# An order of instructions kept as a table in place of a scheduler with offsets

## Chip, core and metric

The kernel runs on one core of a Trainium2 chip. The metric is device time in microseconds (us) of one execution. The core's engines run their own instruction streams side by side: PE (TensorE, matmuls), DVE (VectorE), ACT (ScalarE), POOL (GpSimd) and SP (SyncE, which here issues most DMAs). They wait for one another through semaphores.

## The reference

The kernel computes one layer and its backward pass: the output and the gradients of all eight inputs, for x of 2 batches × 4000 tokens × 144 channels in bfloat16. The forward function:

```python
xa = _layernorm(x)
q, k, v = split(einsum('btd,de->bte', xa, w_qkv))
p = softmax(einsum('btd,bsd->bts', q, k) * D ** (-0.5))
glob = einsum('bts,bsd->btd', p, v) @ w_att_out
u, g = split(gelu(xa @ w_mlp_in))
gc = depthwise_conv5(_layernorm(g), dw_csgu)
loc = (u * gc) @ w_mlp_out
m = concatenate([glob, loc])
m = m + depthwise_conv5(m, dw_merge)
return x + m @ w_merge
```

The attention is full: 4000 × 4000 scores for each batch. `reference` calls `jax.vjp` of this function with `grad_out` and returns the output and all gradients.

## The kernel before

Tokens are handled in 32 blocks of 125 (PB = 125, NB = 32) for each batch. The kernel's stages in order of the span are:

- the head (class `Head`: weights are loaded, transposed and folded together; `pre_pieces`: layer norm of the tokens of batch 0 and transposes, L399 to L446), until about 57 us;
- the attention rows of batch 0 (`phase_att`), 57 to 585 us. For each of the 32 row blocks t it makes the scores S (L1664 with 128 partitions of contraction and L1670 with the remaining 16) in PSUM tiles `ps`, takes each row's minimum and copies the scores out (DVE, L1688 and L1690), takes the exponential (ACT, L1696), transposes it with DMA, and multiplies with V: Y (L1720, 32 matmuls into the PSUM tile `yz`). The DVE and ACT then read `yz`: `rl` (L1726), `dj` (L1729), `nd` (L1731), `yn` (L1733), `ty` (L1736). The gradient of the scores is made from a second product (L1706, or L1709 and L1711), stored transposed by DMA (L1891), and multiplied in Z (L1766, again into a tile `yz`) and X (L1811, accumulated by DVE in L1817). There is one buffer for `yz`. The projections of each row are made ahead of it (`pj`, L1623 to L1629), and their transposes come by DMA (L1646) into `qt`;
- between them, the local branch of the layer (`local_units`, L486 to L690, with matmuls L521 and L522 for the hidden units and L553 and L556 for their gradients), cut into small units;
- the merge of batch 0 (585 to 680 us; weight gradient `Hps` L2096, transposes L2017 and L2022 of reloaded rows `Yg` and `Yr`, outputs `po` L2193 and L2195 with the copies L2196 and the stores L2197), beside which the head pieces of batch 1 run (transposes L399 to L446 again);
- the attention rows of batch 1, until 1210 us, then its merge and the final weight gradients (`pg` L2401, DVE L2408 to L2416, transposes `fpt` L2418, stores L2265, L2414 and L2423).

The Python functions emit all operations in a source order. After that, `Planner.plan` takes the emitted instructions, joins PE instructions that write the same PSUM tile into groups (at most 16; the score matmuls in groups of up to 8), and fixes an order of the groups for each engine. It pins that order by a dependence between each instruction and the next one of its engine:

```python
for e in E:
    prev = None
    for g in order[e]:
        for i in groups[g]["ins"]:
            if prev is not None:
                self.tc.add_manual_dep(i, prev.name, ..., reason="planned order")
            prev = i
```

Before, `order` comes from a list scheduler in `plan`. It holds a duration for every kind of instruction (`cost`), works out which groups must follow which (`region`, `meet`, `under`), and goes through modelled time: whenever an engine is free, it takes among its ready groups the one with the smallest key. The key is the group's place in the source order plus an offset of its kind, `LEAD[tag.engine.tile]`, a list of several hundred numbers.

Matmuls on a zero tile, which nothing reads (`warm`, L153, in `Head.loads`; WARM = 190 of them), have the largest key and so fill moments in which the schedule has no other PE work. They stand from 3 to 57 us of the span.

## Time and profile before

| | before |
|---|---|
| median of 3 runs | 1300.91 us |
| lowest, highest | 1298.82, 1301.12 us |
| profiled execution | 1301.75 us |
| its span | 1299.9 us |
| mean granted TensorE clock | 0.993 |
| instructions in the span | 39018 |
| DMA | 186.53 MB, mean 143 GB/s |

The span is the time between the first and the last record of the profiled execution; its own time is 1.85 us longer. "Busy" is the time in which an engine works; PEld is PE's loading of weights, which overlaps its matmuls. A row of the waits view has the engine and line that waited, the one that released it, the us in total, the number of times and the longest. A row of the timeline has start, duration, engine, line, operation, tiles out and in, and in brackets the idle time before it with its releaser. In the table by stretch, each engine has its busy time and, in brackets, its instructions. The clock is the share of full TensorE speed that was granted.

### The profile page before, as it was taken

The numbers are of one execution on the slowest core, as the hardware profiler recorded it, in microseconds if no ns is written. First come the engines' busy times: TensorE is split into PE (matmuls) and PEld (weight loads), VectorE is DVE, ScalarE is ACT, GpSimd is POOL, SyncE is SP. The second block draws the span as 40 slices with busy tenths as digits, with TensorE's granted clock in tenths as the row PEclk, the third lists the DMA queues.
The fourth block names the chain that finished last, engine by engine and source line by source line (L and its number), as shares of the span: only waits on it lengthen the run. The fifth ranks groups of instructions, "written<-read, shape, count | busy, mean of one in ns | idle before, by whom it ended". The sixth has DMA issues, their size and how long they took to land. (4 is left out here: it accounts for less than half of the span.)

```text
span 1299.9 us, 39018 instructions
## 1 busy us (share of the span) xinstructions
PE 1261.1 (97%) x15888; PEld 1046.4 (80%) x15888; DVE 1051.9 (81%) x2825; ACT 755.4 (58%) x1232; POOL 488.0 (38%) x971
## 2 busy tenths in 40 slices
PE   8999999999999999999999999999999999999996
PEld 7777888778888878888877788888878788878995
DVE  7589888988898978779668988888889798887744
ACT  4766656665566665536645656666565665554471
POOL 8443333444344333313623333434334343222130
PEclk9999999999999999999998999999999999999998
DMA  4499898988989997984249898988898888888511
GB/s 123 79 160 160 157 153 152 146 155 154 154 149 149 157 154 138 171 204 113 74 96 168 150 161 145 155 154 154 143 164 137 159 146 153 157 147 178 162 56 54
DMA packets 630207, 186.53 MB, mean 143 GB/s; under 512 B 612336, under 2 KB 624971, under 8 KB 630021
## 3 DMA queue, kind: packets, MB, share of 16 engines
q1 hardware_dynamic: 629271, 183.57, 78.1%
q8 instruction: 124, 2.03, 0.6%
q14 instruction: 56, 0.46, 0.1%
q0 software_dynamic: 208, 0.25, 0.1%
q10 hardware_dynamic: 548, 0.21, 0.1%
HBM read 20.82 MB, written 14.22 MB: 27 GB/s over the span
## 5 line engine op out<-in xcount | busy, mean ns | idle before, releaser
L1688 DVE TENSOR_SCALAR_CACHE_REDUCE Pb<-ps 125x1000 bf16<-125x1000 f32 x256 | 306.6, 1198 | 82.9 <-PE ps L1670 79.2
L1696 ACT ACTIVATE Pb<-Pb,nm 125x1000 bf16<-125x1000 bf16 x256 | 277.8, 1127 | 104.8 <-DVE nm L1690 104.3
L1811 PE MATMUL X<-SX 125*125 125x144 bf16 x2048 | 294.3, 229 | 3.2 <-ACT l_fl L650 0.9
L1811 PE MATMUL X<-SX,Pb 125*125 125x144 bf16 x2048 | 289.0, 226 | 0.0
L1709 ACT CAST SX<-ps 125x1000 bf16<-125x1000 f32 x189 | 187.8, 994 | 170.8 <-PE ps L1670 168.9
L1811 PEld LDWEIGHTS <-SX 125*125 125x125 bf16 x2048 | 259.0, 137 | 26.9 <-issue 26.7
L1664 PE MATMUL ps<-xaT_m,qt 128*125 128x500 bf16 x1024 | 262.3, 376 | 4.5 <-DVE Pb L1688 2.2
L1811 PEld LDWEIGHTS <-Pb 125*125 125x125 bf16 x2048 | 260.1, 137 | 4.9 <-issue 4.6
L1817 DVE TENSOR_TENSOR acc<-X,acc 125x432 f32<-125x432 f32 x372 | 200.8, 550 | 23.9 <-PE X L1811 21.3
L1766 PE MATMUL yz<-xa_aug,SX 125*125 125x144 bf16 x2048 | 153.0, 230 | 5.9 <-ACT ty L1736 3.7
L1664 PEld LDWEIGHTS <-qt 128*125 128x125 bf16 x1024 | 122.4, 137 | 44.7 <-issue 5.5
L1766 PEld LDWEIGHTS <-SX 125*125 125x125 bf16 x2048 | 141.1, 139 | 13.2 <-issue 9.8
L1720 PE MATMUL yz<-xa_aug,SX 125*125 125x145 bf16 x2048 | 143.4, 228 | 0.9 <-DMA SX<-Pb 0.9
L1711 DVE TENSOR_TENSOR SX<-SX,Pb 125x1024 bf16<-125x1024 bf16 x189 | 132.0, 699 | 13.9 <-ACT SX L1709 9.8
L1720 PEld LDWEIGHTS <-SX 125*125 125x125 bf16 x2048 | 135.7, 137 | 3.6 <-issue 2.0
L1670 PEld LDWEIGHTS <-qt 16*125 16x125 bf16 x1024 | 36.6, 128 | 99.8 <-issue 99.8
L1670 PE MATMUL ps<-XR,qt 16*125 16x500 bf16 x1016 | 112.1, 421 | 0.0
L1706 DVE TENSOR_TENSOR SX<-ps,Pb 125x1000 bf16<-125x1000 f32 x67 | 80.1, 1196 | 11.6 <-ACT SX L1709 8.6
L651 POOL TENSOR_TENSOR A_dwc<-l_fl,A_dwc 128x512 f32<-128x512 f32 (+2 forms) x48 | 37.6, 784 | 97.6 <-ACT l_fl L650 97.5
L1744 POOL TENSOR_SCALAR SX<-qz,rl 125x144 bf16<-125x144 bf16 x62 | 24.3, 392 | 114.9 <-DVE rl L1726 113.4
L1639 POOL COPY qz<-qz 125x48 bf16<-125x48 bf16 x124 | 35.2, 310 | 71.9 <-ACT qz L1629 71.7
L633 POOL TENSOR_SCALAR l_w<-gd,nc,c 125x144 f32<-125x144 bf16 x64 | 29.4, 467 | 83.1 <-DVE c L631 83.0
(485 smaller groups left out, 2334.3 us busy)
## 6 DMA issues: line engine op xcount, KB each, us to landing
go_h<-in_grad_out_dram SPq DMA_DIRECT2D x4, 567.0 KB
Yg<-ug_d SPq DMA_DIRECT2D x4, 567.0 KB
Yn_d<-yn SPq DMA_DIRECT2D x64, 35.2 KB
Zn_d<-qz SPq DMA_DIRECT2D x64, 35.2 KB
ug_d<-ugr SPq DMA_DIRECT2D x32, 70.3 KB
SX<-in_x_dram SPq DMA_DIRECT2D x16, 140.6 KB
out_dram<-Pb SPq DMA_DIRECT2D x16, 140.6 KB
out_dram<-SX SPq DMA_DIRECT2D x16, 140.6 KB
```

Source lines behind the costliest of these rows:

```text
L651: nc.gpsimd.tensor_tensor(acc, fl[0:rows, 0:n], acc, op=ALU.add)
L1664: mm = nc.tensor.matmul(pp[r // 2][:, r % 2, 0:CH], QT[i][:, 3 * h, 0:PB], xaTm[:, c * CH:(c + 1) * CH], start=True, stop=False)
L1670: nc.tensor.matmul(pp[r // 2][:, r % 2, 0:CH], QT[i][rs, 1 + h, 0:PB], xr, start=False, stop=True)
L1688: nc.vector.tensor_scalar(pv(Pbuf, i % NPB, c2), src, -1.0, 3.0e38, op0=ALU.mult, op1=ALU.min, accum_out=NM[i][:, c2:c2 + 1])
L1696: nc.scalar.activation(v, v, ACT.Exp, bias=NM[i][:, 4:5], scale=-1.0)
L1706: nc.vector.tensor_tensor(pv(Sbuf, i % NDB, c2), src, pv(Pbuf, i % NPB, c2), op=ALU.mult)
L1709: nc.scalar.copy(pv(Sbuf, i % NDB, c2), src)
L1711: nc.vector.tensor_tensor(sc, sc, pchunk(i % NPB, c2), op=ALU.mult)
L1720: nc.tensor.matmul(Y, PT[0:PB, j, 0:PB], xaa[:, j, 0:D + 1], start=(j == 0), stop=(j == NB - 1))
L1766: nc.tensor.matmul(Z, ST[0:PB, j, 0:PB], xaa[:, j, 0:D], start=(j == 0), stop=(j == NB - 1))
L1811: nc.tensor.matmul(X[:, jj, :], l, r, start=(n_ == 0), stop=(n_ == len(ops) - 1))
L1817: nc.vector.tensor_tensor(av, X[:, 0:nj, :], av, op=ALU.add)
```

## The change

The scheduler goes: `cost`, `port`, `under`, `region`, `meet`, the table `LEAD` and the constants COLD and RING that it used. In its place stands `ORDER`, which has for each of the five engines the list of its groups in the order in which they are to run. The list is written as differences between the numbers of successive groups. The grouping and the pinning stay as they are. WARM becomes 111 in place of 190. No other operation is added, removed or changed, and the order was found by moving single operations.

```diff
-COLD = 8.5
-WARM = 190
-RING = 230
+WARM = 111
...
-LEAD = {}
+ORDER = {}
 for _s in """
-Fdwct A.Pb:9742 D.Pb:2821 D.jf:-16178 P:-219 S.out_5_dram:13749
-Fdwit A.Pb:2671 D.Pb:-1680 P:1687 S.out_4_dram:8143
...
+PE 10 1 1 1 1 1 1 1 1 1 1 1 1 1 1 1 1 1 1 1 1 1 172 3 -174 1 1 1 174 2 11 -186 ...
...
+    _e, *_v = _s.split()
+    ORDER[_e] = list(itertools.accumulate(int(_a) for _a in _v))
...
-    def plan(self, i0, i1, window=700):
-        import heapq
+    def plan(self, i0, i1):
...
-        key = [g["x"] + LEAD.get(g["cls"], 0.0) + (1e9 if (g["t"] or "")[:4] == "warm" else 0.0) for g in groups]
...
-                    free_t[e] = s + w + G["d"]
...
-        self.groups, self.order, self.times = groups, order, times
+        assert len(groups) == sum(len(v) for v in ORDER.values())
+        order = ORDER
+        for e in E:
+            assert sorted(order[e]) == [x for x, g in enumerate(groups) if g["e"] == e]
+        self.groups, self.order = groups, order
```

Where the two orders differ, set side by side: of the 79 warm matmuls that are gone, 27 stood ahead of the first layer norm transposes L441 (17.34 us in the profile before), 27 stood between 46.02 and 50.21 us, and 25 elsewhere in the head.

## The prediction, made before the changed kernel ran

> **What bounds the kernel now.** I read the busy shares first, then stretches of the span by stage, then the waits of PE (TensorE), and last the timeline at the places where those waits lie. The head of the profile page, and the table by stretch:

> ```profile
> PE 1261.1 (97%) x15888; PEld 1046.4 (80%) x15888; DVE 1051.9 (81%) x2825; ACT 755.4 (58%) x1232; POOL 488.0 (38%) x971
> ```

> ```profile
> core 0: us, PE busy (x) PEld busy (x) DVE busy (x) ACT busy (x) POOL busy (x), PEclk, DMA share, GB/s
> 0.00:57.20 57.20, 53.88 (x469) 43.64 (x470) 37.62 (x111) 36.25 (x81) 37.37 (x104) 1.00 0.38 91
> 57.20:585.00 527.80, 521.64 (x6557) 427.19 (x6557) 446.33 (x1123) 314.87 (x495) 203.20 (x403) 1.00 0.90 157
> 585.00:640.00 55.00, 49.02 (x772) 46.94 (x770) 49.29 (x206) 36.54 (x60) 27.66 (x33) 1.00 0.34 98
> 640.00:680.00 40.00, 38.40 (x498) 32.65 (x496) 22.84 (x54) 18.49 (x31) 12.66 (x24) 1.00 0.37 87
> 680.00:691.50 11.50, 8.04 (x54) 5.43 (x53) 7.52 (x20) 2.17 (x3) 5.25 (x10) 0.70 0.92 171
> 691.50:1210.00 518.50, 510.60 (x6424) 418.14 (x6422) 437.70 (x1087) 306.81 (x473) 187.47 (x380) 1.00 0.89 155
> 1210.00:1285.00 75.00, 74.27 (x1098) 68.71 (x1096) 43.72 (x192) 39.62 (x89) 14.38 (x19) 1.00 0.30 85
> 1285.00:1299.90 14.90, 5.22 (x34) 3.74 (x32) 6.89 (x36) 0.63 (x3) 0.00 (x0) 0.60 0.17 48
> ```

> PE is the bound: 1261.1 of 1299.9 us, so all waiting of PE together is 38.8 us. A new order can win only three things: PE work that goes, PE waits that go, and half-speed stretches that go. The two long stretches of attention rows (57.20 to 585 and 691.50 to 1210) hold little to win: 527.80 − 521.64 = 6.2 and 518.50 − 510.60 = 7.9 us of idle PE, 14.1 together. The rest stands at four joints: the head, the merge of batch 0 (585 to 640), the start of batch 1 (680 to 691.50, clock 0.70) and the tail (clock 0.60). These are the rows of PE's waits that I use:

> ```profile
> PE yz L1766 <- ACT ty L1736: 3.7, 4, 1.7
> ...
> PE fpt L2418 <- DVE Pb L2416: 2.8, 1, 2.8
> PE pm L2017 <- DMA Yg<-Yn_d: 2.4, 1, 2.4
> PE po L2193 <- DVE SX L2196: 2.3, 1, 2.3
> ...
> PE yz L1766 <- DMA SX<-SX: 2.0, 1, 2.0
> PE ps L1664 <- DMA qt<-qz: 1.4, 1, 1.4
> PE pj L1623 <- DVE SX L2196: 1.2, 1, 1.2
> ...
> PE pm L2022 <- POOL Yr L2068: 0.7, 1, 0.7
> ...
> PE pz L2171 <- DVE R L407: 0.6, 1, 0.6
> ...
> PE pt L406 <- DVE R L407: 0.5, 1, 0.5
> ```

> Each is: line that waited, who released it, us in all, times, longest. The profiled execution took 1301.75 us (span 1299.9); the median of the runs is 1300.91, 0.84 less. I sum against 1301.75 and take 0.84 off at the end. A measurement of this kernel can tell about 0.2%, some 2.6 us, from no change.

> **What the change is in the instruction streams.** Both versions emit the same operations and join them into the same groups; only the warm matmuls (L153, which nothing reads) go from 190 to 111. The order is where they differ: outside the longest common order lie 2865 of 15698 PE matmuls, 900 of 2351 DVE, 370 of 1239 ACT, 339 of 971 POOL and 309 of 722 SP instructions. In PE time most matmuls stand within 1 to 3 us of their old place. So I take each joint by itself.

> **1. Seventy-nine warm matmuls fewer (head).**

> ```profile
> 12.11 5.39 PE L153 MATMUL warm<-SX 128*125 128x290 bf16 x42
> 17.34 0.60 PE L441 MATMUL pt<-ident,xa_aug 125*128 125x125 bf16 x8
> ...
> 46.02 4.36 PE L153 MATMUL warm<-SX 128*125 128x290 bf16 x34
> 50.21 0.28 PE L1859 MATMUL pt<-ident,qz 125*128 125x125 bf16 x2
> ```

> ```profile
> 12.83 2.11 DVE L434 TENSOR_SCALAR xa_aug<-SX,rstd_x,acc 125x144 bf16<-125x144 bf16 x4
> ```

> ```profile
> 48.58 0.30 ACT L1855 CAST qz<-pj 125x144 bf16<-125x144 f32 x1
> ```

> 34 warm matmuls hold PE from 46.02 to 50.21: 0.123 us each, so 79 are 9.7 us of PE time. That is a gain only where PE's next real work is ready. Ahead of the first L441 transposes, 27 of the 79 go (3.3 us). Their inputs were ready when L434 ended, 12.83 + 2.11 = 14.94, and PE came to them at 17.34, 2.4 us late; in the new order those four L434 also stand some 15 places earlier on DVE, so I let 3.3 go less 0.5. At 46.02, 7 warm matmuls stand in place of 34: 3.3 us again. The transposes L1859 need the casts L1855, done at 48.88, 1.3 us before PE came; in the new order the casts stand ahead of three exponentials on ACT, so most of the rest goes too; I leave 1.0 us as a new wait, and 0.5 for the 25 others, scattered. Sum: −9.7 + 2.0 = **−7.7**, bounds −9.7 (all was surplus) and −3.7 (2.4 and 1.3, no input earlier, the 25 others nothing).

> The row on the clock that bears on this is in part 3: PE fell to half speed after waits of 1.4 and 2.0 us. [...] What a fall in the head costs is rival B.

> **2. Merge of batch 0 (585 to 640).** PE waited 2.4 us for the reload Yg, then 0.7 for Yr, and idled on copies of the transposes.

> ```profile
> 590.07 0.79 PE L2096 MATMUL Hps<-Yg,go_h 125*128 125x144 bf16 x10
> 590.70 0.29 PE L2096 MATMUL Hps<-Yg,go_r 125*80 125x144 bf16 x2
> 590.82 0.79 PE L2096 MATMUL Hps<-Yg,go_h 125*128 125x144 bf16 x10
> ```

> Twelve matmuls from 590.07 to 590.82: 0.0625 us each. The table puts 54 of these L2096 (other blocks, inputs there already) ahead of the first L2017: 54 × 0.0625 = 3.4 us of work into a wait of 2.4 and the 0.7 behind it, both gone. The work is only moved, so the gain is the waits: −3.1. The DVE copies L407, on which the pz and pt rows waited (0.6 and 0.5), stand earlier on DVE; I take half, −0.5. Sum **−3.6**, bounds 0 (Yg's reload starts later by as much as PE is filled, since SP's order changed too) and −4.2.

> **3. Start of batch 1 (675 to 691.5).**

> ```profile
> 681.68 1.06 PE L1664 MATMUL ps<-xaT_m,qt 128*125 128x500 bf16 x4 [1.43 <-DMA qt<-qz]
> ...
> 685.13 2.21 PE L1766 MATMUL yz<-xa_aug,SX 125*125 125x144 bf16 x16 [2.02 <-DMA SX<-SX]
> 687.13 1.88 PE L1664 MATMUL ps<-xaT_m,qt 128*125 128x500 bf16 x4
> ...
> 689.54 1.75 PE L1766 MATMUL yz<-xa_aug,SX 125*125 125x144 bf16 x16
> ```

> ```profile
> 951.87 1.17 PE L1766 MATMUL yz<-xa_aug,SX 125*125 125x144 bf16 x16 [1.70 <-ACT ty L1736]
> ```

> Sixteen L1766 take 1.17 us at 951.87; here they took 2.21 and 1.75, and four L1664 took 1.88 against 1.06. The half clock thus cost 1.0 + 0.6 + 0.8 = 2.4 us, on top of waits of 1.2 (pj), 1.4 (qt) and 2.0 (Z). In the new order pj (L1623) stands ahead of the 32 L1720 matmuls, 2.0 us earlier in PE time. It can't wait there for the L2196 that released it before: that one now stands on DVE behind rl (L1726), which needs those very L1720, and the kernel would hang. So its buffer comes free earlier. The copy L1629 stands ahead of four exponentials on ACT, and the transposing DMA L1646 four places earlier on SP, past the store L2197 and ahead of both L1891. I count pj's and qt's waits and the half clock as gone and leave Z's wait: 1.2 + 1.4 + 2.4 = **−5.0**, bounds 0 (L1891, now behind L1646 and after a Z that comes earlier, waits as much more) and −7.0 (Z's wait too).

> **4. The two long stretches.** By the new places, about half of the small waits there lose their cause (consumer later or producer earlier), and some fifty other groups of PE come nearer to what feeds them. I see no side that must win: **0**, bounds −14 (all idle PE gone) and +14 (twice the idle). DMA lies near 0.9 in both, so an earlier issue on SP need not land earlier.

> **5. Tail.**

> ```profile
> 1291.63 0.80 DVE L2196 TENSOR_TENSOR SX<-po,SX 125x288 bf16<-125x288 f32 x2
> ...
> 1293.14 0.15 DVE L2416 CAST Pb<-dwm 16x5 bf16<-16x5 f32 x1
> 1293.21 0.44 DVE L2196 TENSOR_TENSOR SX<-po,SX 125x288 bf16<-125x288 f32 x1
> ```

> ```profile
> 1295.09 0.17 PE L2418 MATMUL fpt<-ident,Pb 16*5 16x16 bf16 x1
> ```

> In before, the last 24 output matmuls (L2193/L2195) wait 2.3 us for L2196 copies queued behind the weight gradient's DVE chain, and the last transpose L2418 comes 1.8 us after its input (1293.29 to 1295.09) because PE does those 24 first. In the new order the 24 and their four L2196 stand ahead of that chain: 1.8 + 0.8 us off the end of the chain, 24 × 0.0625 = 1.5 us of matmuls ahead of its start, so −1.1; the output DMA that came last (L2197) is issued early instead, some −0.4. Sum **−1.5**, bounds 0 and −2.5.

> **Sum.** −7.7 − 3.6 − 5.0 + 0 − 1.5 = −17.8. 1301.75 − 17.8 = 1283.95, less 0.84: **1283 us**.

> **Rivals.**

> *A, waits change places.* At each joint another producer comes last a little later (the reload Yg, L1891's pieces, the copies), and only the surplus warm matmuls count: 1301.75 − 7.7 − 0.84 = 1293. For it: many instructions move on every engine, and the DMA queues' share of 0.92 at 680 leaves little room to land earlier. Against it: the moves at the four joints each go at the wait's own releaser. Chance 0.20.

> *B, the head isn't shortened.* The missing warm matmuls become PE waits and the clock halves once. Part 1 gives 0, the price of one half-speed stretch is 2.4: −3.6 − 5.0 − 1.5 + 2.4 = −7.7, again 1293. For it: at 46.02 two waits of over 1 us could stand close together, as at 681. Against it: PE came 2.4 and 1.3 us late. Chance 0.10.

> *C, slower: the handover of yz.* One PSUM tile yz is filled by Y (L1720), then read by rl, dj, nd on DVE and ty (L1736) on ACT, before the next Z (L1766) may write it.

> ```profile
> L1696 ACT ACTIVATE Pb<-Pb,nm 125x1000 bf16<-125x1000 bf16 x256 | 277.8, 1127 | 104.8 <-DVE nm L1690 104.3
> ...
> L1817 DVE TENSOR_TENSOR acc<-X,acc 125x432 f32<-125x432 f32 x372 | 200.8, 550 | 23.9 <-PE X L1811 21.3
> ```

> In the new order 40 of the L1817 stand between rl and nd, against 22: 18 more × 0.55 = 9.9 us; and in 17 of the 64 rows ty comes behind one more exponential, 17 × 1.13 = 19.2 us. If all of it ended as PE waits (29.1, less the 3.7 there now) it would turn −17.8 into +7.6: **1308**. It decides from 17.8/35 = 0.5 us exposed in each of those 35 places. Against it: only 4 of 64 handovers waited in before, with 22 L1817 in the same place, and in 20 other rows ty comes earlier. Chance 0.12.

> *D, nothing comes of it.* The table might pin what the hardware did anyway, gains and losses within the 2.6 us: 1301. The warm matmuls alone speak against it. Chance 0.03.

> **How the numbers follow.** Forecast 0.55, with 1271 to 1291 as its own range (the bounds of its parts, the long stretches at half of theirs). The low end of the whole range is all bounds of parts 1, 2, 3 and 5 with the long stretches at −10: −9.7 − 4.2 − 7.0 − 2.5 − 10 = −33.4, so 1267. The high end takes in A, B and D: 1301; C is left out. Faster: 0.55 + 0.10 + 0.17 of A's 0.20 = 0.82; same: D and 0.02 of A, 0.05; slower: C and 0.01 of A, 0.13.

> **What would show it.** Right: PE's work down by about 9.7 us; no wait over 1.5 us before the first L441 and L1859; no wait of L2017 for Yg; clock 1.00 in the stretch after the first rows of batch 1; L2418 as the last PE step, within 0.3 us of its input. Wrong: idle PE in the long stretches well above 14.1 us, above all L1766 waiting for ty more than 3.7 us (C), or half clock in the head (B), or Yg's and Z's waits as long as before under the same or another name (A).

## The result

The new order runs in 1287.84 us (median of 4 runs, 1286.23 to 1289.86) against 1301.01 us for the kernel before (4 runs): a ratio of 0.9903, 95% interval [0.9883, 0.9922]. Beside the later experiments it was measured once more: 1286.39 us against 1301.50, ratio 0.9886 [0.9873, 0.9899]. The forecast was 1283 us with a range of 1267 to 1301; the gain is 13 to 15 us where 18 were forecast. The profiled execution took 1286.85 us, its span is 1285.1 us, against 1301.75 and 1299.9.

In the changed kernel lines behind the planner are numbered 638 lower (L1766 becomes L1128), lines 434 to 446 one higher (L441 becomes L442), lines 521 to 690 one lower. The head of its profile page:

```profile
PE 1252.2 (97%) x15809; PEld 1037.1 (81%) x15809; DVE 1050.0 (82%) x2825; ACT 760.5 (59%) x1232; POOL 479.7 (37%) x971
```

PE worked 1261.1 − 1252.2 = 8.9 us less, near the 9.7 us of 79 warm matmuls, and its idle time fell from 38.8 to 1285.1 − 1252.2 = 32.9 us.

To see where, I cut both spans at three matmuls that have the same PE instructions ahead of them in both orders, but for the warm ones (a Z matmul in the first rows, an X matmul late in batch 0, a score matmul in the rows of batch 1). The table by stretch, before and then after; the columns are start and end, length, and then for each engine busy time and instructions:

```profile
0.00:62.63 62.63, 59.29 (x534) 47.88 (x534) 41.73 (x124) 38.94 (x88) 42.22 (x113) 1.00 0.43 96
62.63:550.43 487.80, 482.02 (x6006) 391.92 (x6004) 418.29 (x1060) 299.36 (x471) 191.75 (x380) 1.00 0.90 154
550.43:759.64 209.21, 196.67 (x2621) 169.70 (x2619) 165.02 (x488) 113.28 (x179) 79.64 (x138) 0.98 0.65 137
759.64:1299.90 540.26, 523.10 (x6737) 436.94 (x6735) 426.87 (x1157) 303.81 (x496) 174.37 (x341) 0.99 0.78 142
```

```profile
0.00:53.16 53.16, 50.94 (x454) 38.09 (x455) 40.01 (x123) 38.48 (x88) 41.73 (x110) 1.00 0.49 119
53.16:539.63 486.47, 482.42 (x6007) 392.09 (x6004) 418.10 (x1058) 299.89 (x470) 190.20 (x383) 1.00 0.90 153
539.63:750.23 210.60, 197.89 (x2620) 171.54 (x2619) 166.09 (x488) 115.53 (x180) 77.12 (x139) 0.98 0.67 137
750.23:1285.10 534.87, 520.99 (x6738) 435.40 (x6735) 425.76 (x1159) 306.65 (x496) 170.68 (x341) 0.99 0.78 144
```

The head is 9.5 us shorter, the rows of batch 0 1.3 us, the rest of batch 1 with its merge and the tail 5.4 us. The third stretch, with the merge of batch 0 and the start of batch 1, is 1.4 us longer: there the prediction had put 8.6 us of gain.

Of the head's 9.5 us, 2.1 lie at its very start. Before, DVE cleared another tile (`R`) for 1.73 us ahead of the zero tile of the warm matmuls, and PE waited for it; after, the zero tile is the first thing that DVE writes. The wait in the profile before, then DVE before, then DVE after:

```profile
PE warm L153 <- DVE SX L150: 3.3, 1, 3.3
```

```profile
1.23 1.73 DVE L2509 MEMSET R<- 128x2000 uint32 x1 [1.23 <-PEq L2660]
2.96 0.27 DVE L150 MEMSET SX<- 128x256 uint32 x1
```

```profile
0.87 0.27 DVE L151 MEMSET SX<- 128x256 uint32 x1 [0.87 <-PEq L2022]
```

PE's waits in the profile after show what happened in the third stretch:

```profile
PE fpt L1780 <- DVE Pb L1778: 5.2, 2, 2.6
PE yz L1128 <- DMA SX<-SX: 3.3, 5, 1.1
PE po L1555 <- DVE SX L1558: 2.4, 2, 2.0
PE yz L1128 <- ACT ty L1098: 2.2, 3, 1.4
...
PE pt L588 <- DMA gd<-gd: 1.7, 1, 1.7
PE pt L442 <- DVE xa_aug L435: 1.2, 3, 0.6
PE warm L154 <- DVE SX L151: 1.2, 1, 1.2
PE pt L442 <- DVE lnnm L428: 1.1, 1, 1.1
```

The waits for Yg (2.4 us), for qt (1.4) and for pj's buffer (1.2) are gone as forecast. New ones stand near them: the transposes of batch 1's tokens (L442) wait for their layer norm, and an output matmul (L1555) for a copy behind a late load. The timeline of PE at these places:

```profile
609.57 0.60 PE L407 MATMUL pt<-ident,go_r 125*80 125x125 bf16 x8
...
611.03 0.60 PE L400 MATMUL pt<-ident,Pb 125*128 125x125 bf16 x8 [0.74 <-DVE R L447]
612.75 0.61 PE L442 MATMUL pt<-ident,xa_aug 125*128 125x125 bf16 x8 [1.12 <-DVE lnnm L428]
613.20 0.62 PE L446 MATMUL pt<-ident,xa_aug 125*112 125x125 bf16 x8
613.64 1.02 PE L407 MATMUL pt<-ident,go_r 125*80 125x125 bf16 x8
...
651.32 0.76 PE L1555 MATMUL po<-SX 128*125 128x144 bf16 x5 [2.03 <-DVE SX L1558]
```

Eight transposes L407 take 0.60 us at 609.57 and 1.02 at 613.64: the clock fell to half behind the waits (0.50 from 613.66 to 620.48 us). The same at 651.32, where five output matmuls take 0.76 us in place of 0.48 (0.50 from 651.20 to 654.62 us). What this cost can be read from the lead of the new order, that is, how much earlier it starts the same matmul with the same matmuls ahead of it (but for the warm ones). The lead is 10.8 us at 571.23 us of the profile after (582.04 before) and 13.9 at 611.03 (624.89), so 3.0 us were won at Yg. It falls to 10.9 at 620.16 (631.00): 3.0 us lost at the transposes. It falls again from 11.6 at 621.65 (633.22) to 7.9 at 654.57 (662.42): 3.7 us lost at the output matmuls. By 682.27 (693.80) it is back at 11.5, 3.7 us won at the start of batch 1, and in the rows up to the cut at 750.23 (759.64) it falls to 9.4.

### The profile page after: what moved, and what is told of

The parts are those of the page before. It is cut to its first block, busy times and chain, and to the rows that moved or that the text cites. A ratio compares the mean times of both kernels' runs of the same rounds, so it can differ in the third digit from the quotient of the medians.

```text
span 1285.1 us, 38822 instructions
## 1 busy us (share of the span) xinstructions
PE 1252.2 (97%) x15809; PEld 1037.1 (81%) x15809; DVE 1050.0 (82%) x2825; ACT 760.5 (59%) x1232; POOL 479.7 (37%) x971
## 3 DMA queue, kind: packets, MB, share of 16 engines
q8 instruction: 123, 2.02, 0.6%
## 4 chain that ended last, share of the span: by engine, by line
PE 82%; DVE 10%; DMA 3%; issue 1%; ACT 1%; POOL 1%; SPq 0%; DVEq 0%; ACTq 0%; POOLq 0%
PE X L1173 20%; PE ps L1026 15%; PE yz L1128 9%; PE yz L1082 9%; PE ps L1032 6%; PE Hps L1458 4%; PE po L1555 3%; DMA SX<-SX 2%; DVE Pb L1050 2%; DVE acc L1179 1%; PE pj L989 1%; PE pc L607 1%; PE pw L667 1%; PE pd L555 1%; PE pd L622 1%
## 5 line engine op out<-in xcount | busy, mean ns | idle before, releaser
L1058 ACT ACTIVATE Pb<-Pb,nm 125x1000 bf16<-125x1000 bf16 x256 | 278.9, 1127 | 113.5 <-DVE nm L1052 113.2
L1179 DVE TENSOR_TENSOR acc<-X,acc 125x432 f32<-125x432 f32 (+1 forms) x372 | 199.1, 549 | 31.6 <-PE X L1173 29.6
L1128 PE MATMUL yz<-xa_aug,SX 125*125 125x144 bf16 x2048 | 152.1, 228 | 5.8 <-DMA SX<-SX 3.3
L1128 PEld LDWEIGHTS <-SX 125*125 125x125 bf16 x2048 | 139.5, 138 | 13.7 <-issue 7.7
L1001 POOL COPY qz<-qz 125x48 bf16<-125x48 bf16 (+1 forms) x124 | 33.9, 289 | 66.2 <-ACT qz L991 65.4
L1555 PE MATMUL po<-SX 128*125 128x144 bf16 x640 | 54.1, 229 | 2.4 <-DVE SX L1558 2.4
```

Source lines behind the costliest of these rows:

```text
L1058: nc.scalar.activation(v, v, ACT.Exp, bias=NM[i][:, 4:5], scale=-1.0)
L1128: nc.tensor.matmul(Z, ST[0:PB, j, 0:PB], xaa[:, j, 0:D], start=(j == 0), stop=(j == NB - 1))
L1179: nc.vector.tensor_tensor(av, X[:, 0:nj, :], av, op=ALU.add)
L1555: nc.tensor.matmul(po[:, q, :], self.yt(h, i + kk), VU[h][:, kk, :], start=(n_ == 0), stop=False)
```

## The experiments

Where rows of before's profile are compared with another kernel's, the same operation is meant. In each experiment the order of all engines stands in the table; the edits are given as moves in it.

**1. Is the head's gain the missing warm matmuls?** The old order with 79 warm matmuls fewer.

```diff
 PE, old order, head
-42 x L153 ahead of the first L441, 34 x L153 ahead of L1859
+25 x L153 ahead of the first L441,  7 x L153 ahead of L1859
 (and 35 fewer elsewhere; DVE, ACT, POOL, SP as before)
```

> The old order of every engine, written as a table, with the 79 warm matmuls taken out at about the places where the new order has fewer (27 ahead of the first L441, 27 of the 34 ahead of L1859, 25 elsewhere in the head). Theory 'surplus' (the 79 only made PE late; no other move is needed): 9.7 us less, 1301.0 - 9.7 = 1291 us, head ending at about 47.5 us. Theory 'needs the order' (without the earlier casts and layer norm steps the places become PE waits): only 2.4 + 1.3 us and part of the rest, 4 to 6 us less, 1295 to 1297, with new PE waits at L441 and L1859 of about 1 and 2 us.

Measured: 1302.5 us against 1301.48, ratio 1.0010 [1.0000, 1.0021]. Both theories fell: nothing is gained at all. PE did come to the first L442 transposes 2.9 us earlier (14.48 us, against 17.34 for L441 before), only to wait 1.9 us behind them for a copy on DVE (L447). PE's timeline and the clock in this kernel:

```profile
47.18 0.28 PE L1216 MATMUL pt<-ident,qz 125*128 125x125 bf16 x2 [3.13 <-ACT qz L996]
...
58.18 1.99 PE L1077 MATMUL yz<-xa_aug,SX 125*125 125x145 bf16 x22
```

```profile
50.00:55.00 5.00, 5.00 (x18) 2.26 (x16) 1.80 (x2) 3.23 (x7) 0.67 (x1) 0.50 0.00 0
```

PE stands at the transposes of qz from 44.05 us, waits 3.13 us for the cast behind the exponentials, and then runs for some 10 us at half clock (the clock, third column from the end, is 0.50 between 50 and 55 us). The first Y starts at 58.18 us; in before it was 57.22. All the work taken out came back as waits and as half clock (a stretch of 10.2 us from 48.88 us on). This is the prediction's rival B, in the old order.

**2. The casts alone.** The kernel of experiment 1 with one edit on ACT.

```diff
 ACT, 43 to 61 us of the old profile
-exp, ..., exp, exp, cast L1855, exp, copy L1639, ...
+exp, ..., cast L1855, copy L1639, ..., exp, ..., exp, ..., exp
```

> The old order with 111 warm matmuls (1302.5 us, a wait of 3.1 us at the transposes L1859 and half clock until 59 us), with one more edit: among the ACT operations of 43 to 61 us of the old profile, the casts L1855 and L1639 stand ahead of the first block's exponentials, as in the new order. Theory 'casts' (PE's 3.1 us wait is the cast behind the exponentials, the half clock its consequence): both go, 3.1 + 4.4 us, 1295 us. Theory 'exponentials' (their delay makes the transposes of P and the first Y late): the wait only moves to the first Y (L1720), 1300 to 1302.

Measured: 1295.58 us against 1301.48, ratio 0.9958 [0.9942, 0.9975]: the casts' theory. The first Y and the clock:

```profile
52.41 2.19 PE L1077 MATMUL yz<-xa_aug,SX 125*125 125x145 bf16 x32
```

```profile
50.00:55.00 5.00, 4.94 (x60) 3.81 (x59) 3.14 (x7) 4.53 (x12) 1.92 (x5) 1.00 0.32 60
```

The first Y comes 5.8 us earlier than in experiment 1, and the clock is 1.00 between 45 and 60 us. This kernel still has the late zero tile, as the old order has.

**3. The other engines' order in the head, PE's left as it was.**

```diff
 head (until 61 us of the old profile), 111 warm matmuls
-DVE, ACT, POOL, SP: old order
+DVE, ACT, POOL, SP: new order
 PE: old order
```

> The old order with 111 warm matmuls (1302.5 us), but DVE, ACT, POOL and SP in the new order until 61 us of the old profile; PE keeps the old order in the head. Theory 'producers' (the head was set by the order of the other engines, which the warm matmuls only covered): as the whole new head, 1292 to 1293 us. Theory 'both' (PE must also come to the early inputs early): halfway to the casts alone, 1294 to 1296, with PE waits of 1 to 2 us between 12 and 30 us.

Measured: 1293.31 us against 1301.50, ratio 0.9944 [0.9932, 0.9956]. With the new order of PE as well (next experiment) it is 1293.15. The first Y starts at 49.06 us here and at 47.24 there:

```profile
49.06 2.19 PE L1077 MATMUL yz<-xa_aug,SX 125*125 125x145 bf16 x32
```

So the producers carry most of the head's gain, the earlier zero tile among their moves; PE's own order adds 1.8 us at the first Y, and in the time of the runs nothing that can be told.

**4. The new order in the head alone, and behind it alone.**

```diff
 kernel a: groups until 61 us of the old profile
-old order, 190 warm matmuls
+new order, 111 warm matmuls
 kernel b: all groups
-new order, 111 warm matmuls
+new order, 190 warm matmuls
```

> The new order with 111 warm matmuls until the first Y matmuls of batch 0 (61 us in the old profile), the old order behind it on all engines. Theory 'additive': 1301.0 - 9.4 = 1291.6 us, that is all of the head's gain and nothing else. Theory 'spread' (the head's gain is partly lost in waits of the old order behind it, which was set for the later start): 1294 or more.

> The new order of every engine with 79 warm matmuls put back into the head. Theory 'additive' (the head and the rest are separate): 1287.8 + 9.5 = 1297 us, so the order behind the head is worth about 4 us. Theory 'warm only' (the order behind the head is worth nothing): 1301.

Measured: 1293.15 us for the head alone, ratio 0.9929 [0.9917, 0.9941]; 1296.6 us for the new order with 190 warm matmuls, ratio 0.9964 [0.9951, 0.9977]. The head alone is worth some 8 to 9 us, between its two theories. Kernel b has the time of the additive theory, but its gain of 4.9 us isn't all from behind the head, since it has the new order in the head too, and with it the earlier zero tile. Its first Y matmuls come 2.1 us before the old order's (57.22 us), with all 190 warm matmuls in place:

```profile
55.09 1.23 PE L1083 MATMUL yz<-xa_aug,SX 125*125 125x145 bf16 x16
```

In the changed kernel, with 111, they come at 47.09 us. So the same removal of 79 warm matmuls that gave nothing in the old order (experiment 1) is worth 8.0 us at the first Y in the new one, and 9 to 10 us in the time of the runs. What lies behind the head is better read from kernel a against the whole change: 1293.15 against 1287.84 or 1286.39, so 5 to 7 us.

**5. The merge of batch 0 and the start of batch 1 alone.**

```diff
 groups between 547 and 757 us of the old profile
-old order
+new order
 (elsewhere the old order, 190 warm matmuls)
```

> The old order with 190 warm matmuls, but the new order between 547 and 757 us of the old profile (end of batch 0's rows, its merge, the start of batch 1). The prediction's parts 2 and 3 would give 3.6 + 5.0 us: 1292.4. Theory 'given back' (from the two traces: 3.6 won at Yg, 2.8 lost at the transposes of batch 1's tokens, 3.7 lost at a late load of x ahead of the output matmuls, 2.4 won at the start of batch 1): 0 to 1 us slower than before, 1301 to 1302.

Measured: 1305.67 us against 1301.48, ratio 1.0036 [1.0023, 1.0049]: not a gain, and worse than "given back" had it. By the lead in the section on the result, the four amounts of that theory are rather 3.0, 3.0, 3.7 and 3.7 us. The loss beyond it fits one wait that neither before nor after has at this size:

```profile
715.50 3.40 PE L1079 MATMUL yz<-xa_aug,SX 125*125 125x145 bf16 x32 [3.48 <-DMA SX<-Pb]
```

Y waits 3.48 us for the transposing DMA and then takes 3.40 us for 32 matmuls that take 2.19 in experiment 2; the X matmuls behind start 0.12 us apart until 719.66 us, and 0.06 us apart from there on, so the stretch ran at half clock. The counterpart, the new order with the old one put back in this stretch:

```diff
 groups between 547 and 757 us of the old profile
-new order
+old order
 (elsewhere the new order, 111 warm matmuls)
```

> The new order, but with the old order between 547 and 757 us of the old profile. Theory 'given back': 1 to 4 us less than the new order, 1284 to 1287. Theory 'the order there is needed by what follows' (the later rows were set for the new start of batch 1): 1288 or more.

Measured: 1286.39 us, ratio 0.9881 [0.9863, 0.9900], which can't be told from the new order (0.9886 and 0.9903). In its profile the waits for Yg (2.7 us), Z (1.9), qt (1.3) and pj (1.2) are all back, at no cost in time. So this stretch contributes nothing to the gain, and that the old order is better there is not shown either.

**6. The late load.**

```diff
 SP, new order
-load x for piece 5; load x for piece 4
+load x for piece 4; load x for piece 5
```

> The new order with one edit: the load of x for output piece 4 (L1547 on SP, 645.56 us in the profile after) stands ahead of the load for piece 5, which waited until 645.18, as in the old order. Theory 'queue' (the output matmuls wait 2.0 us at 651 since that load was issued late, and the clock falls to half for 3 us): 2.0 + 1.7 us less than the new order, 1284 us. Rival 'DVE' (the copy L1558 is behind the 1.2 us row minimum anyway): at most 1 us less, 1287.

Measured: 1286.28 us, ratio 0.9882 [0.9866, 0.9897]: no difference from the new order that can be told. The wait at the output matmuls did fall, from 2.03 to 0.92 us, but in this execution the clock fell at 622 us in place of 613 (1.00 from 605 to 620 us, 0.73 between 620 and 625):

```profile
622.26 3.78 PE L1533 MATMUL pz<-xa_aug,Pb 125*128 125x144 bf16 x32 [0.99 <-DVE R L408]
```

(the same 32 matmuls took 2.16 us in the profile after).

**7. POOL beside DVE in the layer norm.** At 612.75 and 615.76 us of the profile after, DVE's step L435 takes about 1.3 us where the median of 16 such steps is 0.32. First DVE, then POOL:

```profile
612.75 1.69 DVE L435 TENSOR_SCALAR xa_aug<-Pb,rstd_x,lnnm 125x144 bf16<-125x144 bf16 x2
...
615.76 1.37 DVE L435 TENSOR_SCALAR xa_aug<-Pb,rstd_x,lnnm 125x144 bf16<-125x144 bf16 x1
```

```profile
612.66 1.27 POOL L1586 TENSOR_TENSOR Pb<-t,go_h 125x576 bf16<-125x576 f32 x1
...
615.81 1.27 POOL L1586 TENSOR_TENSOR Pb<-t,go_h 125x576 bf16<-125x576 f32 x1
```

Each slow step ends within 0.1 us of the end of POOL's product (the first of the two in the row at 612.75 lasts 1.25 us).

```diff
 POOL, new order
-L437 (group 2), L1586 (piece 2), 4 x L437 (group 3)
+L437 (group 2), 4 x L437 (group 3), L1586 (piece 2)
```

> The new order with one edit: on POOL the product L1586 of piece 2 stands behind the four layer norm steps L437 of the last group. Theory 'collision' (at 612.7 and 615.8 us the DVE step L435 takes 1.3 us in place of 0.3 because POOL runs an L1586 of 1.3 us beside it): L435 takes 0.3 us there, the waits of the transposes L442 (2.7 us in all) fall by 1 to 2 us and the half clock of 613 to 620 us goes, 2 to 4 us less than the new order, 1284 to 1286. Rival (the chain of layer norm steps is late on POOL itself, by rstd_x L424): no change, 1288.

Measured: 1285.71 us, ratio 0.9877 [0.9862, 0.9892]. The first collision is gone, the second stayed:

```profile
615.54 1.06 DVE L435 TENSOR_SCALAR xa_aug<-Pb,rstd_x,lnnm 125x144 bf16<-125x144 bf16 x1
```

Of the 2 to 4 us expected some 2 show at most (0.7 against the new order's later median), and the interval overlaps the new order's, so a gain isn't shown.

**8. Both repairs and the rest of that chain; then the tail.** The new order once more beside them.

```diff
 kernel a: the edits of 6 and 7, and
 POOL
-L1586, 3 x L437 (group 2), rstd_x L424 (group 3)
+L1586, rstd_x L424 (group 3), 3 x L437 (group 2)
 DVE
-copies L447, L408, L447 between the four L435 of group 3
+four L435 of group 3 ahead of the copy L447 that follows
 kernel b: kernel a, and in the tail (PE, with DVE, ACT and SP to match)
-7 pieces of po between the last transposes of HT and the first pg L1763
+4 pieces of po there, the others beside the DVE chain of pg
```

> The new order unchanged, for the comparison with the repairs beside it: 1288 us; its profile shows again the half clock at 613 to 620 and at 651 to 655 us.

> The new order with both repairs (the load of x first; POOL's product L1586 behind the layer norm steps) and two more moves in the same place: POOL takes rstd_x of the last group (L424) ahead of the steps L437 of the group before, and DVE its four steps L435 ahead of the copies of the transposes. Theory 'chain' (the transposes of batch 1's tokens wait for that chain only): waits of L442 and L446 below 1 us in all, no half clock between 605 and 660 us, 4 to 5 us less than the new order: 1283 to 1284. Rival 'clock' (the waits left still stand close enough together to halve the clock somewhere behind them): 1285 to 1286.

> f4_merge with one more move: in the tail the chain of the last weight gradient (pg L1763, DVE L1770 to L1778, transposes L1780) starts some 3 us earlier, with output matmuls beside it. If the end is this chain: 2 to 4 us less than f4_merge, 1280 to 1281. If the output matmuls and their stores take its place as the last: no change.

Measured: the new order 1286.39 us, ratio 0.9886 [0.9873, 0.9899], with the half clock not where it was expected (last section); kernel a 1283.02, 0.9859 [0.9847, 0.9872]; kernel b 1281.02, 0.9839 [0.9826, 0.9852]. The repairs together gain 3.4 us. The tail gains 2 more; the intervals of a and b overlap, but each of the four runs of b is below each of the four of a. So kernel b beats both kernels, by 20 us the one before. Kernel a has the time that its chain theory gave, but not the two conditions: the four steps L435 of the last group do take 1.09 us together, yet of the transposes' waits the two below are left, and the clock still falls (0.73 between 615 and 620 us).

```profile
613.53 1.09 DVE L435 TENSOR_SCALAR xa_aug<-Pb,rstd_x,lnnm 125x144 bf16<-125x144 bf16 x4
```

```profile
611.64 0.60 PE L400 MATMUL pt<-ident,Pb 125*128 125x125 bf16 x8 [0.64 <-DVE R L447]
613.66 0.60 PE L442 MATMUL pt<-ident,xa_aug 125*128 125x125 bf16 x8 [1.42 <-DVE R L408]
```

The last transposes of the tail, in kernel a and kernel b:

```profile
1276.20 0.17 PE L1780 MATMUL fpt<-ident,Pb 16*5 16x16 bf16 x1 [2.60 <-DVE Pb L1778]
```

```profile
1273.92 0.17 PE L1780 MATMUL fpt<-ident,Pb 16*5 16x16 bf16 x1 [2.68 <-DVE Pb L1778]
```

In both it waits 2.6 to 2.7 us for DVE and nothing follows on PE: the end is still this chain.

## Why the prediction came out

**Part 1, the head: about the right size, with one step wrong and one wait left out.** Forecast −7.7, the profiles show −9.5, of which 2.1 are the earlier zero tile: a wait of 3.3 us, the second longest row of PE's waits before, that the prediction did not use. But the step failed that read "2.4 us late" at L441 and "1.3 us before PE came" at L1859 as time to be won, with −3.7 as the least: experiment 1 took the warm matmuls out with no input earlier and gained nothing (+1.0 us, interval 0.0 to +0.2%). That PE is late at one matmul does not mean that the head is PE's. Behind each place stood copies on DVE and casts on ACT that PE only reached sooner to wait longer, and half clock came behind the waits (10.2 us of it in experiment 1). The moves on DVE and ACT that the prediction named beside them were no addition to that gain but its condition (experiments 2 to 4): the producers' order makes the gain, and the smaller number of warm matmuls lets it through.

**Part 2, Yg: the waits won as forecast, then given back.** The waits for Yg and Yr were put at −3.1, and the lead grows by 3.0. 54 blocks of Hps moved into the wait of Yg, and it is gone. The layer norm chain behind did not come as much earlier, so that the transposes, with their waits and the half clock, took 3.0 us more. This is rival A, at a place that the prediction had counted as a gain of half a microsecond.

**Part 3, start of batch 1: forecast −5.0, in the profile −3.7, and not kept.** qt's and pj's waits are gone, and Z still waits (0.8 and 1.1 us in place of 2.0), as forecast. New is a wait of 1.7 us for the reload gd (L588), and 2.1 us of the lead go again in the rows behind. The clock between 655 and 685 us was 1.00 in the profile after, but in the second profile of the same kernel it was 0.50 from 679.75 to 683.16 (last section). What parts 2 and 3 left out is the loads of x on SP behind the moves: 3.7 us lost at 651. Parts 2 and 3 together, −8.6, measured +1.4, and experiment 5 finds the same time with the old order back in this stretch.

**Part 4, the long stretches: forecast 0, measured −1.3 in batch 0 and −4.6 in batch 1.** The last stretch, cut once more where both orders have the same PE instructions ahead, before and then after:

```profile
759.64:1237.50 477.86, 471.11 (x6016) 389.76 (x6015) 397.74 (x1043) 277.63 (x430) 164.17 (x333) 1.00 0.86 153
1237.50:1299.90 62.40, 51.98 (x725) 47.18 (x722) 29.14 (x114) 26.18 (x68) 10.20 (x8) 0.90 0.20 57
```

```profile
750.23:1223.47 473.24, 470.11 (x6016) 389.41 (x6014) 394.93 (x1042) 279.46 (x429) 160.12 (x331) 1.00 0.86 154
1223.47:1285.10 61.63, 50.88 (x725) 45.98 (x722) 30.83 (x117) 27.19 (x68) 10.56 (x10) 0.92 0.21 60
```

In the rows of batch 1 idle PE fell from 6.8 us to 3.1, in waits of at most 1.7 us each, and PE's own work by 1.0 us. The runs say the same: the kernel of experiment 5 with the old order only between 547 and 757 us takes 1286.39 us, and the one of experiment 4 with the new order in the head alone 1293.15, so the long rows and the tail bring 6.8 us. The prediction had seen that about half of the small waits lose their cause, set against it some fifty groups that come nearer to what feeds them, and put the sum at 0; those groups cost less than the others gained. What share of the 4.6 us each wait has wasn't tried one by one.

**Rival C did not happen:** Z waits for ty 2.2 us in three places against 3.7 in four, with the L1817 between rl and nd that the prediction counted.

**Part 5, the tail: forecast −1.5, measured −0.8** (62.40 and 61.63 us, rows above). L1780 came as the last PE step, 0.05 us behind its input, as forecast:

```profile
1279.79 0.16 DVE L1778 CAST Pb<-dwm 16x5 bf16<-16x5 f32 x1
```

```profile
1280.00 0.17 PE L1780 MATMUL fpt<-ident,Pb 16*5 16x16 bf16 x1 [2.60 <-DVE Pb L1778]
```

But the wait of 2.3 us for the L2196 copies came back as a second wait of 2.6 us for the DVE chain: the waits for it are 2.8 us in one before and 5.2 in two after. What is won is PE's own work, 1.1 us less: the last output matmuls no longer run at half clock (five of them take 0.48 us, 0.76 to 0.80 in before).

That the sum lies near the forecast is luck: the earlier zero tile in the head and a gain in the long rows, neither of which its sum had, made up for most of the 8.6 us that parts 2 and 3 did not bring.

## What to carry to other kernels

A wait that is filled with work from further on is won only if what that work used to cover is covered otherwise: look at the next joint, too. Filler on the bounding engine that seems to overrun can stand on another engine's chain; take it out and look where the engine waits next, before counting its time as a gain. Where waits of 1 to 3 us stand close together, count the half clock behind them at several microseconds of uncertainty (3.0 and 3.7 us of the lead were lost at two such places here), and compare orders by runs, not by one profile. Read every long row of the waits, at the start of the span too: here the first memset of DVE was worth 2.1 us.

## What the runs showed of the hardware

```profile
647.79:651.20 3.41, 1.50 (x24) 1.42 (x23) 1.87 (x4) 3.41 (x5) 1.79 (x4) 1.00 0.31 94
651.20:654.61 3.41, 3.29 (x26) 3.10 (x26) 0.07 (x1) 0.86 (x1) 0.00 (x0) 0.50 0.55 126
```

```profile
649.03:652.44 3.41, 1.66 (x27) 1.57 (x25) 1.10 (x3) 2.91 (x3) 0.55 (x2) 1.00 0.31 108
652.44:655.85 3.41, 3.41 (x38) 2.51 (x37) 1.55 (x3) 0.99 (x1) 0.00 (x0) 1.00 0.98 116
676.33:679.75 3.42, 1.45 (x21) 1.33 (x22) 3.07 (x7) 0.16 (x1) 0.80 (x2) 1.00 0.60 116
679.75:683.16 3.41, 3.41 (x20) 2.25 (x17) 0.00 (x0) 1.49 (x4) 1.02 (x4) 0.50 1.24 223
```

Behind a window with PE busy for 1.50 us of 3.41 the clock is halved, and so behind one with 1.45; behind one with 1.66 it isn't, though PE's longest wait at that place is nearly the same in both executions (2.0 and 1.8 us). With the profiles before and after cut on their grids from 8 us on, windows at full clock in which PE was busy for 1.02 and 1.42 us (before) and for 0.78, 1.50 and 1.55 us (after) had half clock behind them; no other window at full clock did, and the least busy of the others had 1.71 us (950.08 us in before) and 1.75 us (678.51 in after). The grid lies elsewhere in the second execution (a window starts at 649.03 us there and at 647.79 in the first), so the same waits are cut differently. Waits of 2.0 us with work before and behind (651.32 us in after), and one of 3.13 us (experiment 1), were enough for half clock.

**Slow DVE steps ended with a POOL product.** In the profile after, L435 took 0.31 us at 601.00 us, with POOL idle, and 1.37 at 615.76 beside L1586 of 1.27 us. That step and the first at 612.75 us end within 0.1 us of the end of POOL's product (experiment 7), and with the first product moved the two steps at 613.28 us took 0.62 us together. Which of the two came first can't be read there: at 615.76 us the record of the DVE step starts 0.05 us ahead of POOL's.
